# First two token tiles loaded by rows beside weight pairs on two DMA queues, and turned by TensorE, with a shorter warm-up

## Chip, cores and metric

One Trainium2 chip, one core. The metric is the device time of one execution in microseconds; lower is better. Differences of a few tenths of a per cent are the subject here, so every experiment was timed in five rounds next to the kernel before, on the same chip (except one, a single look). The groups ran on six different chips, so a comparison between groups is weaker than one within a group.

## The reference, cut to what matters

Two attention blocks read the same token matrix `x` of 2048 x 1024 (bfloat16); their outputs are mixed by a gate. Only the start matters here: the first product that the kernel forms is the value part of block B.

```python
qkv = (x @ wqkv).reshape(B, S, 3, H, Dh)...   # x: 2048 x 1024, wqkv: 1024 x 3072
q, k, v = qkv[0], qkv[1], qkv[2]              # block B's v needs x and wqkv[:, 2048:3072]
# block A: linear attention; block B: sliding, dilated window of 8; both end in @ wo
return g * a + (1 - g) * b
```

## The kernel before

Each real matmul of the opening multiplies a stationary 128 x 128 block by 512 columns (`128*128 128x512` in the profile). The kernel takes 128 tokens of `x` as the stationary block, with the features along the partitions, so it needs `x` turned: tile `xT[:, :, t*128:(t+1)*128]`. The kernel brings each of the 16 tiles by a DMA that transposes on its way. The weights of `v` come in two halves of 512 columns, and each half as four pairs of feature blocks ("weights 0-1" to "6-7", 256 KB each).

A small scheduler inside the kernel's builder orders all operations on each engine by planned costs. The scheduler's times only fix the order.

```python
WARM = 11          # matmuls on zeros, to bring TensorE's clock up

def load_x(t, prio):          # one tile of 128 tokens, transposed by the DMA
    ... e.dma_start_transpose(xT[:, :, t*128:(t+1)*128], x2[e_, r*128:(r+1)*128, :]) ...

load_x(0, 0)
load_w(0, 0, Bw, 2048, 0.1, 0, 2, "act")     # weights 0-1, ScalarE's queue
load_w(0, 0, Bw, 2048, 0.2, 2, 4, "act")
load_w(0, 0, Bw, 2048, 0.3, 4, 6)            # SyncE's queue
load_w(0, 0, Bw, 2048, 0.4, 6, 8)
for t in range(1, NT):
    load_x(t, 3 + t)
for d in range(0, 8, 2):                     # second half of the weights
    load_w(0, 1, Bw, 2560, 6.1 + 0.1 * d, d, d + 2)
# ... (cut)
for i in range(WARM):
    P.op("pe", lambda e: e.matmul(banks[7].ap(), warm[:, 0:128], warm[:, :], start=True, stop=True), 0.43, ...)
# ... (cut)
# tiles 0-3 with the first half, tiles 0-3 with the second half, tiles 4-7, ...
for t, half in [(4 * b + i, half) for b in range(NT // 4) for half in range(2) for i in range(4)]:
    step = 2 if t == 0 else 8                # tile 0 starts pair by pair
    for d in range(0, 8, step):
        o = group(bank, xs, w, [xr, ws[0].part((d, d + step), ...)], d, d + step)
    # ... eviction to SBUF and store to HBM (cut)
```

Masks for block B's window are made at the start by GpSimd and copied by VectorE; they are needed much later. The warm-up matmuls came 0.43 us apart at first, and the dense part later runs at 0.2155 us each.

Of the kernel before, what the change touches and what calls it, by code (L numbers as in the profile page):

```python
# [62 lines left out]
class Prog:  # L63
# [58 lines left out]
    def schedule(self, dma_rate=0.2e6):  # L122
        for o in self.ops:
            for d in o.deps:
                d.users.append(o)
        left = {o: len(o.deps) for o in self.ops}
        ready_at = {o: 0.0 for o in self.ops}
        free = {e: 0.0 for e in self.ENGS}
        dma_free = 0.0
        wait = {e: [] for e in self.ENGS}  # L130
        avail = {e: [] for e in self.ENGS}

        def ready(o, at):
            if o.eng == "any":

                est = []
                for e in ("act", "dve"):
                    q = sum(x[2].cost for x in avail[e] if x[0] < o.prio) + sum(x[2].cost for x in wait[e] if x[2].prio < o.prio and x[0] < at + 0.3)
                    est.append((max(free[e], at) + q + o.cost[e], e))
                o.eng = min(est)[1]  # L140
                o.fn, o.cost = o.fn[o.eng], o.cost[o.eng]
            heapq.heappush(wait[o.eng], (at, o.seq, o))

        for o in self.ops:
            if left[o] == 0:
                ready(o, 0.0)
        self.order = {e: [] for e in self.ENGS}
        mode = "m"
        done = 0
        while done < len(self.ops):  # L150
            best = None
            for e in self.ENGS:
                while wait[e] and wait[e][0][0] <= free[e]:
                    _, _, o = heapq.heappop(wait[e])
                    heapq.heappush(avail[e], (o.prio, o.seq, o))
                if avail[e]:
                    t = free[e]
                elif wait[e]:
                    t = wait[e][0][0]
                else:  # L160
                    continue
                if best is None or t < best[0]:
                    best = (t, e)
            assert best is not None, "no operation can go"
            t, e = best
            if not avail[e]:
                while wait[e] and wait[e][0][0] <= t:
                    _, _, o = heapq.heappop(wait[e])
                    heapq.heappush(avail[e], (o.prio, o.seq, o))
            _, _, o = heapq.heappop(avail[e])  # L170
            if e == "pe":

                if o.mode != mode and mode != "m":
                    near = [x for x in avail[e] if x[2].mode == mode and x[0] < o.prio + 30]
                    if near:
                        x = min(near)
                        avail[e].remove(x)
                        heapq.heapify(avail[e])
                        heapq.heappush(avail[e], (o.prio, o.seq, o))
                        o = x[2]  # L180
                if o.mode != mode:
                    t += 0.09
                mode = o.mode
            o.start = t
            o.end = t + o.cost
            free[e] = o.end
            fin = o.end
            if o.chan is not None:
                dma_free = max(dma_free, o.end) + o.lat
                fin = dma_free + o.pad  # L190
            o.pos = len(self.order[e])
            self.order[e].append(o)
            done += 1
            for u in o.users:
                lat = self.LAT[o.eng] if (u.eng != o.eng or o in u.raw) and o.chan is None else 0.0
                if u.eng == o.eng == "pe":
                    lat = 0.0
                ready_at[u] = max(ready_at[u], fin + lat)
                left[u] -= 1
                if left[u] == 0:  # L200
                    ready(u, ready_at[u])
        self.span = max(free.values())
# [914 lines left out]
def build_kernel(nc, A_x, A_wqkv, A_wo, B_x, B_wqkv, B_wo, gate_w, out):  # L1117
# [10 lines left out]
    def SB(shape, dtype, name, at=None):  # L1128
        n = SZ[dtype]
        for d in shape[1:]:  # L1130
            n *= d
        if at is None:
            at = base[0]
            base[0] += (n + 31) // 32 * 32
        uid[0] += 1
        h = nc.alloc_sbuf_tensor_at("%s_%d" % (name, uid[0]), list(shape), dtype, offset=at)
        return Tile("S", h, at, list(shape), dtype)
# [80 lines left out]
    warm = SB([128, 512], BF16, "warm", at=pk.t[2].lo)  # L1218
    gwb = SB([128, 1024], BF16, "gwb", at=pk.t[3].lo)
    xn = Ring([SB([128, 1024], BF16, "xn%d" % i, at=az.t[i].lo) for i in range(2)])  # L1220
    top_ = base[0]
    base[0] = ph
    osb = Ring([SB([128, 1024], BF16, "o%d" % i) for i in range(2)])
# [4 lines left out]

    FILL = 0.2
    PVLAG = 3  # L1230
    WARM = 11
    PASSES = 6
    mm = lambda n: max(n / 2400.0, 0.0267) + 0.0025
    act = lambda n: 0.19 + n / 1200.0
# [2 lines left out]
    def plan(seen):  # L1237
# [25 lines left out]
        def C(eng, fn, cost, writes, reads=()):  # L1263
            return P.op(eng, fn, cost, reads=reads, writes=writes, prio=-1)

        for z in vst.t:
            C("pool", lambda e, z=z: e.memset(z[:, :, 32:33], 1.0), 0.1, [z.part((0, 16), (32, 33))])
        C("pool", lambda e: e.memset(eps[:], 1e-6), 0.1, [eps.all()])
        for i, (n, offs) in enumerate(KINDS):
            for h, o in enumerate(offs):  # L1270
                m = mtmp[h]
                b0 = o + 64 * h
                C("pool", lambda e, m=m: e.memset(m[:], 1.0), 0.1, [m.all()])

                C("pool", lambda e, m=m, n=n, b0=b0: e.affine_select(out=m[:, :, 0:n], in_=m[:, :, 0:n], compare_op=ALU.is_ge, fill=0.0, base=b0,
                                                                     pattern=[[0, 2], [1, n]], channel_multiplier=-1), 0.3, [m.all()], [m.all()])
                C("pool", lambda e, m=m, n=n, b0=b0: e.affine_select(out=m[:, :, 0:n], in_=m[:, :, 0:n], compare_op=ALU.is_ge, fill=0.0, base=7 - b0,
                                                                     pattern=[[0, 2], [-1, n]], channel_multiplier=1), 0.3, [m.all()], [m.all()])
                C("dve", lambda e, m=m, n=n, h=h, i=i: e.tensor_copy(msk[i][64 * h:64 * h + 64, :, :], m[64 * h:64 * h + 64, :, 0:n]), 0.2, [msk[i].all()], [m.all()])
                P.ops[-1].prio = 1100  # L1280
        C("pool", lambda e: e.memset(zsel[:], 0.0), 0.3, [zsel.all()])

        C("dve", lambda e: e.memset(warm[:, :], 0.0), 0.15, [warm.all()])
# [22 lines left out]
        def load_x(t, prio):  # L1306
            e_, r = t // 8, t % 8
            return P.op("sp", lambda e: e.dma_start_transpose(xT[:, :, t * 128:(t + 1) * 128], x2[e_, r * 128:(r + 1) * 128, :]),  # L1308
                        1.5, writes=[xT.part((0, 8), (t * 128, (t + 1) * 128))], prio=prio, chan="x%d" % t, lat=1.3)
# [3 lines left out]
            return P.op(eng, lambda e: e.dma_start(ws[slot][:, d0:d1, half * 512:half * 512 + 512], src[:, d0:d1, c0:c0 + 512]), 0.4 + 0.2 * n,  # L1313
                        writes=[ws[slot].part((d0, d1), (half * 512, half * 512 + 512))], prio=prio, chan="w%d_%d_%d" % (slot, half, d0), lat=0.55 * n, after=after)

        load_x(0, 0)
        load_w(0, 0, Bw, 2048, 0.1, 0, 2, "act")
        load_w(0, 0, Bw, 2048, 0.2, 2, 4, "act")
        load_w(0, 0, Bw, 2048, 0.3, 4, 6)
        load_w(0, 0, Bw, 2048, 0.4, 6, 8)  # L1320
        for t in range(1, NT):
            load_x(t, 3 + t)
        for d in range(0, 8, 2):
            load_w(0, 1, Bw, 2560, 6.1 + 0.1 * d, d, d + 2)
        P.op("sp", lambda e: e.dma_start(gwb[:, :], gate_w[None, :].to_broadcast([128, D])), 0.6, writes=[gwb.all()], prio=29, chan="gw", lat=0.8)
# [46 lines left out]
        for i in range(WARM):  # L1372
            P.op("pe", lambda e: e.matmul(banks[7].ap(), warm[:, 0:128], warm[:, :], start=True, stop=True), 0.43, reads=[warm.all()], writes=[banks[7].iv], prio=-1)


        early = {(2, 0): (1, 0, Bw, 1024, 21), (4, 1): (2, 0, Bw, 0, 22), (7, 1): (1, 1, Bw, 1536, 23), (10, 1): (2, 1, Bw, 512, 24),
                 (12, 1): (3, 0, Aw, 1024, 25), (14, 1): (3, 1, Aw, 1536, 26)}
        for t, half in [(4 * b + i, half) for b in range(NT // 4) for half in range(2) for i in range(4)]:
            vt, vs = vst.next()
            xs, xr = x_tile(t)  # L1380
            bank = main.next()
            w, wr = w_half(0, half)
            step = 2 if t == 0 else 8
            for d in range(0, 8, step):
                o = group(bank, xs, w, [xr, ws[0].part((d, d + step), (half * 512, half * 512 + 512))], d, d + step)
            move(vt[:, :, 0:32], lambda bank=bank: bank.ap().rearrange("p (h d) -> p h d", d=32), 512, bank, vt.part((0, 16), (0, 32)))
            P.op("sp", lambda e, t=t, vt=vt, half=half: e.dma_start(vB_hbm[t * 128:(t + 1) * 128, half * 528:half * 528 + 528], vt[:, :, :].rearrange("p h d -> p (h d)")), 0.6, reads=[vt.all()],
                 writes=[hb(t * 128, (t + 1) * 128, half)], chan="vst%d" % vs, lat=0.5, prio=5)
            if (t, half) in early:
                load_w(*early[t, half], after=[o])  # L1390
        load_w(0, 0, Aw, 2048, 30)
        load_w(0, 1, Aw, 2560, 31)

# [424 lines left out]
```

## Time and profile before

| | before |
|---|---|
| median of the first three runs | 486.72 us (486.56 to 486.83) |
| span of the profiled run | 485.2 us |
| TensorE busy | 474.2 us |
| first real matmul | 5.54 us |
| TensorE almost without a stop from | 15.30 us |

From the page of the profile before: the span, busy time of the engines, and the shares of the chain of waits that ended last, by engine.

```profile
span 485.2 us, 10105 instructions
PE 474.2 (98%) x4339; PEld 222.8 (46%) x4403; DVE 285.2 (59%) x547; ACT 140.2 (29%) x227; POOL 5.9 (1%) x36
PE 95%; SPq 2%; issue 1%; DMA 1%; ACT 0%; DVE 0%
```

The same chain in order of time (start, duration, what). "SPq" is issuing on SyncE's queue. The chain reaches TensorE at 15.30 us and, but for short pieces, stays there; the line at 129.63 is the first score matmul, a landmark that has 568 matmuls of 512 columns ahead of it.

```profile
9.96 5.07 DMA w<-in_B_wqkv_dram
...
15.30 10.74 PE ps_all L1334 x49
...
129.63 0.53 PE ps_all L1440 x32
```

TensorE's timeline before (start, duration, engine, line, operation, operands, count; in brackets the idle time just before the group and what ended it). A group that runs on past the end of the view is cut there, as the last one here. L1373 is the warm-up, L1334 real work.

```profile
1.25 4.01 PE L1373 MATMUL ps_all<-warm 128*128 128x512 bf16 x11 [1.25 <-DVE warm L1283]
5.54 1.47 PE L1334 MATMUL ps_all<-w,xT 128*128 128x512 bf16 x6 [0.28 <-DMA xT<-in_A_x_dram]
7.25 0.60 PE L1334 MATMUL ps_all<-w,xT 128*128 128x512 bf16 x2 [0.24 <-DMA w<-in_B_wqkv_dram]
8.17 6.82 PE L1334 MATMUL ps_all<-w,xT 128*128 128x512 bf16 x30 [0.32 <-DMA xT<-in_A_x_dram]
15.30 2.97 PE L1334 MATMUL ps_all<-w,xT 128*128 128x512 bf16 x13 [0.30 <-DMA w<-in_B_wqkv_dram]
```

The first tile's transpose ends the first wait, weights end the next, and the second tile's transpose the one at 8.17. In the dense part one matmul takes about 0.2155 us, so 38 of them ahead of 15.30 us correspond to a gapless start at 15.30 - 38 x 0.2155 = 7.1 us. This "effective start" is the figure that a better opening has to lower.

SyncE's issue timeline before. A transpose holds the queue for 1.38 us and, in the group of three, for 1.6 us on average; the second half of the weights is therefore issued only from 8.31 us.

```profile
0.80 1.38 SPq L1308 DMA_TRANSPOSE xT<-in_A_x_dram  x1
2.24 1.06 SPq L1313 DMA_DIRECT2D w<-in_B_wqkv_dram  x2
3.35 4.92 SPq L1308 DMA_TRANSPOSE xT<-in_A_x_dram  x3
8.31 2.12 SPq L1313 DMA_DIRECT2D w<-in_B_wqkv_dram  x4
```

### The profile page before, as it was taken

How to read it: one execution, taken by the hardware profiler on the slowest of the kernel's cores; microseconds unless marked ns; L12 is line 12 of the kernel's file. 1: busy time of each engine (PE TensorE's matmuls, PEld its weight loads, DVE VectorE, ACT ScalarE, POOL GpSimd, SP SyncE). 2: the span in 40 equal slices, each digit the busy share in tenths (PEclk: the TensorE clock that was granted, in tenths of full speed). 3: DMA queues.
4: the chain of work that ended last, by engine and by line, in shares of the span. 5: the costliest groups of instructions: out<-in, count | busy, mean ns of one | idle time of the engine just before them, and what ended most of it. 6: DMA issues, size and time to landing. Idle time of an engine off the chain costs nothing.

```text
span 485.2 us, 10105 instructions
## 1 busy us (share of the span) xinstructions
PE 474.2 (98%) x4339; PEld 222.8 (46%) x4403; DVE 285.2 (59%) x547; ACT 140.2 (29%) x227; POOL 5.9 (1%) x36
## 2 busy tenths in 40 slices
PE   8999999999999999999999999999999999999997
PEld 3444444444444444454544554444444444444443
DVE  2121435888688888665666556496579236653434
ACT  2111121235322234334443333455532230111000
POOL 4000000000000000000000000000000000000000
PEclk9999999999999999999999999999999999999999
DMA  8999993132014459433222322820086018830212
GB/s 224 222 194 299 309 355 122 65 110 86 1 44 135 107 138 245 100 76 86 55 75 67 85 66 66 204 54 2 10 217 163 1 15 242 221 24 2 88 68 89
DMA packets 72951, 57.39 MB, mean 118 GB/s; under 512 B 37953, under 2 KB 60865, under 8 KB 72898
## 3 DMA queue, kind: packets, MB, share of 16 engines
q1 hardware_dynamic: 72210, 56.07, 44.3%
q8 instruction: 36, 0.59, 0.5%
q10 hardware_dynamic: 688, 0.59, 0.4%
q14 instruction: 17, 0.14, 0.1%
HBM read 34.49 MB, written 13.76 MB: 99 GB/s over the span
## 4 chain that ended last, share of the span: by engine, by line
PE 95%; SPq 2%; issue 1%; DMA 1%; ACT 0%; DVE 0%
PE ps_all L1334 78%; PE ps_all L1693 11%; PE ps_all L1463 2%; PE ps_all L1440 2%; SPq L1308 1%; DMA w<-in_B_wqkv_dram 1%; PE ps_all L1556 1%; SPq L1313 1%; PE ps_all L1638 0%; PE ps_all L1610 0%; ACT e L1341 0%; DVE o L1697 0%
## 5 line engine op out<-in xcount | busy, mean ns | idle before, releaser
L1334 PE MATMUL ps_all<-w,xT 128*128 128x512 bf16 x924 | 208.6, 379 | 4.5 <-issue 2.1
L1334 PE MATMUL ps_all<-xT,w 128*128 128x512 bf16 x745 | 166.3, 379 | 2.2 <-issue 1.4
L1334 PEld LDWEIGHTS ps_all<-w,xT 128*128 128x128 bf16 x960 | 91.2, 98 | 111.1 <-DMA w<-in_B_wqkv_dram 2.1
L1334 PEld LDWEIGHTS ps_all<-xT,w 128*128 128x128 bf16 x768 | 73.9, 98 | 88.7 <-issue 1.3
L1693 PE MATMUL ps_all<-w,qT 128*128 128x512 bf16 (+1 forms) x260 | 55.4, 372 | 0.2
L1693 PEld LDWEIGHTS ps_all<-w,qT 128*128 128x128 bf16 x264 | 25.9, 98 | 29.6
L1365 DVE CAST vst<-ps_all 128x512 bf16<-128x512 f32 x15 | 10.4, 694 | 43.5 <-PE ps_all L1334 43.5
L1448 ACT ACTIVATE E<-ps_all 128x1824 bf16<-128x1824 f32 (+1 forms) x18 | 30.4, 1689 | 13.4 <-PE ps_all L1440 13.4
L1345 DVE TENSOR_SCALAR e<-e 128x512 bf16<-128x512 bf16 x64 | 18.4, 290 | 26.9 <-ACT e L1343 14.0
L1697 DVE SCALAR_TENSOR_TENSOR o<-ps_all,gm,xT 128x512 bf16<-128x512 f32 (+1 forms) x25 | 18.0, 728 | 21.1 <-PE ps_all L1693 20.8
L1341 ACT ACTIVATE e<-ps_all 128x512 bf16<-128x512 f32 x32 | 19.1, 598 | 39.0 <-PE ps_all L1334 38.1
L1343 ACT ACTIVATE e<-ps_all 128x512 bf16<-128x512 f32 x32 | 19.1, 598 | 32.3 <-PE ps_all L1334 32.3
L1295 DVE TENSOR_TENSOR mx<-mx,kT 128x1024 bf16<-128x1024 bf16 x32 | 20.9, 688 | 10.9 <-ACT kT L1366 10.8
L1295 DVE TENSOR_TENSOR mx<-mx,qT 128x1024 bf16<-128x1024 bf16 x32 | 20.8, 687 | 7.9 <-ACT qT L1369 7.9
L1451 DVE TENSOR_TENSOR E<-E,msk 128x1824 bf16<-128x1824 bf16 (+1 forms) x18 | 19.9, 1104 | 7.8 <-ACT E L1448 7.4
L1366 ACT ACTIVATE vst<-ps_all 128x512 bf16<-128x512 f32 x17 | 10.2, 601 | 48.5 <-PE ps_all L1334 45.1
L1480 DVE TENSOR_TENSOR ot<-ps_all,rs 128x512 bf16<-128x512 f32 x36 | 23.3, 686 | 0.0
L1366 ACT ACTIVATE az<-ps_all 128x512 bf16<-128x512 f32 x22 | 13.2, 601 | 34.5 <-PE ps_all L1334 34.5
L1366 ACT ACTIVATE kT<-ps_all 128x512 bf16<-128x512 f32 x20 | 11.9, 597 | 37.6 <-PE ps_all L1334 37.6
L1347 DVE SCALAR_TENSOR_TENSOR pk<-ps_all,e 128x512 bf16<-128x512 f32 x32 | 22.0, 689 | 0.7
L1369 ACT ACTIVATE qT<-ps_all 128x512 bf16<-128x512 f32 x19 | 11.4, 598 | 37.4 <-PE ps_all L1334 37.3
L1369 ACT ACTIVATE xT<-ps_all,g 128x512 bf16<-128x512 f32 x10 | 6.9, 689 | 45.1 <-PE ps_all L1334 45.1
(72 smaller groups left out, 260.2 us busy)
## 6 DMA issues: line engine op xcount, KB each, us to landing
rb<-rc_hbm SPq DMA_DIRECT2D x32, 256.0 KB, 5.2
w<-in_A_wqkv_dram SPq DMA_DIRECT2D x6, 1024.0 KB, 9.0
v<-vB_hbm SPq DMA_DIRECT2D x36, 132.0 KB, 2.7
vB_hbm<-vst SPq DMA_DIRECT2D x32, 132.0 KB, 6.2
w<-in_B_wqkv_dram SPq DMA_DIRECT2D x4, 1024.0 KB, 9.5
xn<-in_A_x_dram SPq DMA_DIRECT2D x16, 256.0 KB, 2.7
out_dram<-o SPq DMA_DIRECT2D x15, 256.0 KB, 2.1
oB_hbm<-ot SPq DMA_DIRECT2D x36, 96.0 KB, 2.2
```

Of the source, the lines that this page charges most:

```text
L1295: P.op("dve", lambda e, m=m, op=op: e.tensor_tensor(m[:, 0:n], m[:, 0:n], src, op), 0.08 + n / 1920.0, reads=[m.all(), reg], writes=[m.all()],
L1334: last = e.matmul(bank.ap(), lhs(dc), rhs(dc), start=(dc == 0), stop=(dc == 7))
L1341: P.op("act", lambda e: e.activation(e_[:, :], bank.ap(), ACT.Exp), act(512), reads=[bank.iv], writes=[e_.all()])
L1343: P.op("act", lambda e: e.activation(e_[:, :], bank.ap(), ACT.Exp, accum_out=qe[:, col:col + 1]), act(512) + 0.1, reads=[bank.iv], writes= ...
L1345: P.op("dve", lambda e: e.tensor_scalar(e_[:, :], e_[:, :], 1.0, 1e-6, op0=ALU.min, op1=ALU.add), 0.25, reads=[e_.all()], writes=[e_.all()])
L1347: P.op("dve", lambda e: e.scalar_tensor_tensor(out=dst, in0=bank.ap(), scalar=0.0, in1=e_[:, :], op0=ALU.max, op1=ALU.add), dps(512), read ...
L1366: fa = lambda e: e.activation(dst, src(), ACT.Copy)
L1369: fa = lambda e: e.activation(dst, src(), ACT.Copy, scale=scale)
L1448: P.op("act", lambda e: e.activation(E[:, 0:32 * nq].rearrange("p (j q) -> p j q", j=4), ps[:, 4:8, 0:8 * nq], ACT.Exp), act(32 * nq), rea ...
L1451: P.op("dve", lambda e: e.tensor_tensor(ev(), ev(), m[:, :, :].rearrange("p r q -> p (r q)")[:, None, :].to_broadcast([128, 16, 2 * nq]), ...
L1480: P.op("dve", lambda e, r=r, bv=bv, h=h: e.tensor_tensor(o[:, 512 * h:512 * h + 512].rearrange("p (k i c) -> p k i c", k=2, c=32), bv()[:, ...
L1693: last = e.matmul(bank.ap(0, f1 - f0), qT[:, dc, t * 128:(t + 1) * 128], ws[3][:, dc, f0:f1], start=(dc == 0), stop=(dc == 7))
```

## The change

The intent is to start the real work earlier. The first two tiles are loaded plainly, by rows, and TensorE turns them itself: it multiplies each 128 x 128 block by an identity matrix, and ScalarE and VectorE copy the result from PSUM into `xT`. Row loads and weight pairs go in two queues side by side. The masks are made later, so that GpSimd can make the identity first. Because real work is expected earlier, the warm-up has six matmuls instead of eleven, and one more between the two tiles' turns. The core of the diff:

```diff
-    WARM = 11
+    WARM = 6
@@
-        load_x(0, 0)
-        load_w(0, 0, Bw, 2048, 0.1, 0, 2, "act")
-        load_w(0, 0, Bw, 2048, 0.2, 2, 4, "act")
-        load_w(0, 0, Bw, 2048, 0.3, 4, 6)
-        load_w(0, 0, Bw, 2048, 0.4, 6, 8)
-        for t in range(1, NT):
-            load_x(t, 3 + t)
+        due(load_rows(0, 0, 1024, 0, "act"), 0.45, 3.0)
+        due(load_w(0, 0, Bw, 2048, 0.1, 2, 4, "act"), 0.45, 4.6)
+        due(load_w(0, 0, Bw, 2048, 0.2, 6, 8, "act"), 0.45, 6.2)
+        due(load_w(0, 0, Bw, 2048, 0.1, 0, 2), 0.45, 3.0)
+        due(load_rows(1, 0, 1024, 0.2), 0.45, 4.6)
+        due(load_w(0, 0, Bw, 2048, 0.3, 4, 6), 0.45, 6.2)
+        for t in range(2, NT):
+            o = load_x(t, 3 + t)
+            if t < 4:
+                due(o, 1.4, 7.6 + 1.2 * (t - 2))
@@
+        for t, p in [(t, p) for t in range(2) for p in range(4)]:
+            b = banks[3 + p]
+            def turn(e, t=t, b=b, p=p):
+                for k in range(2):
+                    d = 2 * p + k
+                    last = e.matmul(b.ap(128 * k, 128 * k + 128), rows_[t][:, d * 128:(d + 1) * 128], ident[:, :], ...)
+                return last
+            o = P.op("pe", turn, 0.18, ...)
+            ... copy to xT by VectorE (p even) or ScalarE (p odd)
+            for i in range({3: 1}.get(4 * t + p, 0)):    # one more warm-up matmul
+                P.op("pe", ... warm ..., after=[o])
@@
-            step = 2 if t == 0 else 8
+            step = 2 if t == 0 or t == 1 and half == 0 else 8
@@
   (cut: the identity; the masks moved to after the 17th group; planned landing times for the scheduler)
```

`due` only tells the scheduler when a load is expected; it sets the order, not a wait.

More of the change, by code (lines that the diff above doesn't have):

```diff
@@ L188, in schedule @@
             if o.chan is not None:
-                dma_free = max(dma_free, o.end) + o.lat
-                fin = dma_free + o.pad
+                if o.lat is None:
+                    fin = max(o.end + 1.2, o.pad)
+                else:
+                    dma_free = max(dma_free, o.end) + o.lat
+                    fin = dma_free + o.pad
             o.pos = len(self.order[e])
@@ L1220, in build_kernel @@
     xn = Ring([SB([128, 1024], BF16, "xn%d" % i, at=az.t[i].lo) for i in range(2)])
+    rows_ = [SB([128, 1024], BF16, "rows%d" % i, at=az.t[2 + i].lo) for i in range(2)]
+    ident = SB([128, 128], BF16, "ident", at=er.t[0].lo)
     top_ = base[0]
@@ L1264, in C @@
             return P.op(eng, fn, cost, reads=reads, writes=writes, prio=-1)
+        C("pool", lambda e: e.memset(ident[:, :], 0.0), 0.1, [ident.all()])
+        C("pool", lambda e: e.affine_select(out=ident[:, :], in_=ident[:, :], compare_op=ALU.not_equal, fill=1.0, base=0, pattern=[[-1, 128]], channel_multiplier=1), 0.3,
+          [ident.all()], [ident.all()])
         for z in vst.t:
@@ L1268, in plan @@
         C("pool", lambda e: e.memset(eps[:], 1e-6), 0.1, [eps.all()])
-        for i, (n, offs) in enumerate(KINDS):
-            for h, o in enumerate(offs):
-                m = mtmp[h]
-                b0 = o + 64 * h
-                C("pool", lambda e, m=m: e.memset(m[:], 1.0), 0.1, [m.all()])
-                C("pool", lambda e, m=m, n=n, b0=b0: e.affine_select(out=m[:, :, 0:n], in_=m[:, :, 0:n], compare_op=ALU.is_ge, fill=0.0, base=b0,
-                                                                     pattern=[[0, 2], [1, n]], channel_multiplier=-1), 0.3, [m.all()], [m.all()])
-                C("pool", lambda e, m=m, n=n, b0=b0: e.affine_select(out=m[:, :, 0:n], in_=m[:, :, 0:n], compare_op=ALU.is_ge, fill=0.0, base=7 - b0,
-                                                                     pattern=[[0, 2], [-1, n]], channel_multiplier=1), 0.3, [m.all()], [m.all()])
-                C("dve", lambda e, m=m, n=n, h=h, i=i: e.tensor_copy(msk[i][64 * h:64 * h + 64, :, :], m[64 * h:64 * h + 64, :, 0:n]), 0.2, [msk[i].all()], [m.all()])
-                P.ops[-1].prio = 1100
         C("pool", lambda e: e.memset(zsel[:], 0.0), 0.3, [zsel.all()])
@@ L1314, in load_w, with load_rows, due @@
                         writes=[ws[slot].part((d0, d1), (half * 512, half * 512 + 512))], prio=prio, chan="w%d_%d_%d" % (slot, half, d0), lat=0.55 * n, after=after)
-        load_x(0, 0)
-        load_w(0, 0, Bw, 2048, 0.1, 0, 2, "act")
-        load_w(0, 0, Bw, 2048, 0.2, 2, 4, "act")
-        load_w(0, 0, Bw, 2048, 0.3, 4, 6)
-        load_w(0, 0, Bw, 2048, 0.4, 6, 8)
-        for t in range(1, NT):
-            load_x(t, 3 + t)
+        def load_rows(t, lo, hi, prio, eng="sp"):
+            return P.op(eng, lambda e: e.dma_start(rows_[t][:, lo:hi], x2[0, t * 128:(t + 1) * 128, lo:hi]), 0.45, writes=[rows_[t].part((lo, hi))], prio=prio, chan="xr%d_%d" % (t, lo))
+        def due(o, cost, at):
+            o.cost, o.lat, o.pad = cost, None, at
+        due(load_rows(0, 0, 1024, 0, "act"), 0.45, 3.0)
[8 more added lines that the diff above has]
+                due(o, 1.4, 7.6 + 1.2 * (t - 2))
         for d in range(0, 8, 2):
@@ L1373, in plan @@
             P.op("pe", lambda e: e.matmul(banks[7].ap(), warm[:, 0:128], warm[:, :], start=True, stop=True), 0.43, reads=[warm.all()], writes=[banks[7].iv], prio=-1)
+        for t, p in [(t, p) for t in range(2) for p in range(4)]:
[3 more added lines that the diff above has]
+                    d = 2 * p + k
+                    last = e.matmul(b.ap(128 * k, 128 * k + 128), rows_[t][:, d * 128:(d + 1) * 128], ident[:, :], start=(k == 0), stop=(k == 1), skip_group_check=True)
+                return last
+            o = P.op("pe", turn, 0.18, reads=[rows_[t].part((256 * p, 256 * p + 256)), ident.all()], writes=[b.iv], prio=-0.5 + 0.01 * p)
+            src = lambda b=b: b.ap(0, 256).rearrange("p (k s) -> p k s", k=2)
+            dst = xT[:, 2 * p:2 * p + 2, t * 128:(t + 1) * 128]
+            fn = (lambda e, dst=dst, src=src: e.activation(dst, src(), ACT.Copy)) if p % 2 else (lambda e, dst=dst, src=src: e.tensor_copy(dst, src()))
+            P.op("act" if p % 2 else "dve", fn, act(256) if p % 2 else dps(256), reads=[b.iv], writes=[xT.part((2 * p, 2 * p + 2), (t * 128, (t + 1) * 128))], prio=3 + 0.01 * p)
+            for i in range({3: 1}.get(4 * t + p, 0)):
+                P.op("pe", lambda e: e.matmul(banks[7].ap(), warm[:, 0:128], warm[:, :], start=True, stop=True), 0.43, reads=[warm.all()], writes=[banks[7].iv], prio=-0.4, after=[o])
         early = {(2, 0): (1, 0, Bw, 1024, 21), (4, 1): (2, 0, Bw, 0, 22), (7, 1): (1, 1, Bw, 1536, 23), (10, 1): (2, 1, Bw, 512, 24),
@@ L1382, in plan @@
             w, wr = w_half(0, half)
-            step = 2 if t == 0 else 8
+            step = 2 if t == 0 or t == 1 and half == 0 else 8
             for d in range(0, 8, step):
-                o = group(bank, xs, w, [xr, ws[0].part((d, d + step), (half * 512, half * 512 + 512))], d, d + step)
+                o = group(bank, xs, w, [xT.part((d, d + step), (t * 128, (t + 1) * 128)), ws[0].part((d, d + step), (half * 512, half * 512 + 512))], d, d + step)
             move(vt[:, :, 0:32], lambda bank=bank: bank.ap().rearrange("p (h d) -> p h d", d=32), 512, bank, vt.part((0, 16), (0, 32)))
@@ L1388, in plan @@
                  writes=[hb(t * 128, (t + 1) * 128, half)], chan="vst%d" % vs, lat=0.5, prio=5)
+            if (t, half) == (8, 0):
+                first = o
             if (t, half) in early:
                 load_w(*early[t, half], after=[o])
+        for i, (n, offs) in enumerate(KINDS):
+            for h, o in enumerate(offs):
+                m = mtmp[h]
+                b0 = o + 64 * h
+                P.op("pool", lambda e, m=m: e.memset(m[:], 1.0), 0.1, after=[first], writes=[m.all()])
+                P.op("pool", lambda e, m=m, n=n, b0=b0: e.affine_select(out=m[:, :, 0:n], in_=m[:, :, 0:n], compare_op=ALU.is_ge, fill=0.0, base=b0,
+                                                                     pattern=[[0, 2], [1, n]], channel_multiplier=-1), 0.3, writes=[m.all()], reads=[m.all()])
+                P.op("pool", lambda e, m=m, n=n, b0=b0: e.affine_select(out=m[:, :, 0:n], in_=m[:, :, 0:n], compare_op=ALU.is_ge, fill=0.0, base=7 - b0,
+                                                                     pattern=[[0, 2], [-1, n]], channel_multiplier=1), 0.3, writes=[m.all()], reads=[m.all()])
+                P.op("dve", lambda e, m=m, n=n, h=h, i=i: e.tensor_copy(msk[i][64 * h:64 * h + 64, :, :], m[64 * h:64 * h + 64, :, 0:n]), 0.2, writes=[msk[i].all()], reads=[m.all()])
         load_w(0, 0, Aw, 2048, 30)
```

## The prediction

> **What bounds the kernel now.** The page gives PE 474.2 of 485.2 us busy, and the chain of waits that ended last is 95% PE. In order of time, the chain's first 15.3 us are DMA issues on SP, then a weight DMA; from 15.30 us on it is PE, almost without a break. So only the opening can give time.
>
> In the PE timeline the first real matmul starts at 5.54 us, when the first DMA transpose lands. Further stops: 6.4 and 7.25 (weight pairs), 8.17 (second transpose), 14.38 and 15.02-15.30 (the second half's last pairs). 38 loads precede the last stop, so the 39th matmul starts at 15.30. At the dense rate (about 0.2155 us per 512-column matmul) this equals a gapless stream begun at 15.30 - 38 x 0.2155 = 7.1 us. I call this the effective start.
>
> Why it is late: in the SP issue timeline a transpose costs 1.25 to 2.27 us of issue and a plain load about 0.46. The second half's weights are issued only at 8.31-10.4, and the DMA rate falls under 100 GB/s around 9.6-10.8 us. Bytes start at about 2.1 us and move at 307 GB/s in 3-6 us and 258 in 6-9 us.
>
> **What the change does.** It takes two DMA transposes from the head of SP's queue and puts three plain loads on each of two queues (1.57 MB), then two transposes, then the second half's weights at about 4.9-6.9 us, 3.4 us earlier than now. [...] It adds 16 small TensorE turns (about 1 us), eight evictions of 256 columns (an estimate of 0.35-0.45 us each, from 0.60-0.69 us for 512), and moves the mask work of POOL and DVE to about 35 us, where PSUM banks give slack. PE's order after the opening is unchanged.
>
> **Cost on the path.** Estimate at 307 GB/s: the last first-half weights land at about 7.2-7.6 us, with 8 to 10 matmuls ahead of them: effective start 5.3-5.8. The third tile's transpose lands near 8.8, 16 matmuls ahead: 5.4. The second half's last pair lands at 13.3-14.5, 38 ahead: 5.1-6.3. I take 5.7, a gain of 1.4 us.
>
> Clock: six warm-up matmuls end near 3.8 us; before, the eleven changed pace from 0.43 to about 0.21 us at about 4.4. [...] Some first matmuls may now run at 0.43 us; part of that hides under DMA.
>
> **Predicted: 485.3 us, 8 in 10 between 484.4 and 486.4.** Chances: faster by over 2% 0.005, within 2% 0.99, slower by over 2% 0.005.
>
> **Right or wrong in the profile.** First real matmuls at about 5 us; first-half weights landed by 7.6; no wait for second-half weights over 0.3 us; no DMA trough near 10 us; 39th matmul at 13.5-14.2 instead of 15.30; after it, the same PE stretches shifted by a constant 1.4 us. Wrong: weight stops at 12-15 us, loads under 280 GB/s, matmuls at 0.43 us after 5 us.
>
> **What would make it wrong.** The clock stays low past 7 us (loses up to 1.5 us); two queues share so that all pairs land late together; evictions or the identity delay the turns; evictions queueing behind masks near 35 us; or bytes flow better than I think (gain over 2 us).

The sum takes 307 GB/s, the rate of the kernel before from 3 to 6 us, for both queues together (an estimate); the effective start goes from 7.1 to 5.7 us, a gain of 1.4 us, and 486.7 - 1.4 = 485.3 us.

## The result

| | before | changed |
|---|---|---|
| median, six runs each | 486.49 us | 487.73 us |
| range | 486.21 to 486.83 | 487.03 to 488.82 |
| ratio | | 1.0026, interval 1.0011 to 1.0041 |
| first real matmul (profiled run) | 5.54 us | 6.23 us |
| first score matmul | 129.63 us | 131.08 us |
| span of the profiled run | 485.2 us | 486.7 us |

A ratio is the mean time of one kernel's runs over the mean of the other's runs of the same rounds, so it is not quite the ratio of the medians. The ratios for the experiments come out when the first round, the one that was profiled, is left out of these means. The change is slower by 0.26%, inside the 2% band, and outside the predicted range.

The changed kernel's own runs already hint at something: three lie at 487.0 to 487.2 and three at 488.2 to 488.8, while before spreads over 0.6 us.

From the page of the changed kernel: span, busy time, the granted TensorE clock in 40 slices (tenths), and the chain's shares by engine.

```profile
span 486.7 us, 10207 instructions
PE 481.6 (99%) x4415; PEld 224.6 (46%) x4415; DVE 291.1 (60%) x557; ACT 137.9 (28%) x225; POOL 6.6 (1%) x38
PEclk9999999999999999999999999999999999999999
PE 98%; DMA 1%; DVE 0%; issue 0%
```

Its chain in order of time, from the first DMA to the landmark (L1387 are the turns, L1395 the extra warm-up matmul, L1339 real work, L1475 the first score matmul).

```profile
0.80 4.06 DMA rows<-in_A_x_dram
...
4.99 1.01 PE ps_all L1387 x8
6.00 0.43 PE ps_all L1395
6.43 0.85 PE ps_all L1339 x2
7.29 0.85 PE ps_all L1387 x8
8.14 122.94 PE ps_all L1339 x566
131.08 0.53 PE ps_all L1475 x32
```

The landmark came 131.08 - 129.63 = 1.45 us later than before, and the whole span is 1.5 us longer. So everything was lost in the opening, and nothing afterwards. After the first tile's rows landed at 4.9 us, the chain stays on TensorE to the landmark and beyond: TensorE is the slow part. (The chain's start of a group, 6.43 us here, counts from the end of the matmul before; the timeline, from which the table's 6.23 is taken, shows the overlapping start.) Two real matmuls took 0.85 us, twice the dense pace. The weight loads show how long that lasted (the fourth column names PE's weight loader; one load goes with each matmul, 4415 of both in the page above):

```profile
8.36 0.15 PEld L1339 LDWEIGHTS ps_all<-w,xT 128*128 128x128 bf16 x1 [0.28 <-issue]
8.79 0.15 PEld L1339 LDWEIGHTS ps_all<-w,xT 128*128 128x128 bf16 x1 [0.28 <-issue]
9.22 0.15 PEld L1339 LDWEIGHTS ps_all<-w,xT 128*128 128x128 bf16 x1 [0.28 <-issue]
9.62 0.96 PEld L1339 LDWEIGHTS ps_all<-w,xT 128*128 128x128 bf16 x5 [0.26 <-issue]
```

Loads come 0.43 us apart up to 9.62 us, then five within 0.96 us. TensorE ran at half rate until 9.6 us. Note that the clock row above shows 9 in every slice all the same: the trace's record of the clock begins only with the rise (at 9.58 us here, at 4.24 us before), and the stretch before it is drawn as full. The pace of the instructions shows the truth.

SyncE's issue timeline after. The two transposes held the queue for 5.67 us, 3.19 us of it the second one, so the second half of the weights was issued at 8.01 us.

```profile
2.30 5.67 SPq L1304 DMA_TRANSPOSE xT<-in_A_x_dram  x2
8.01 2.12 SPq L1309 DMA_DIRECT2D w<-in_B_wqkv_dram  x4
```

Landing times of the opening's loads, as issue time plus time to landing of each in the trace: rows 0 at 4.9, weights 0-1 at 5.3, weights 2-3 at 6.8, rows 1 at 6.9, weights 6-7 at 8.1 and 4-5 at 8.4 us.

Busy time and DMA rate in two stretches, first of the kernel before, then of the changed one. The columns are the stretch, its length, the busy time of PE, PEld, DVE, ACT and POOL with the instruction counts in brackets, the granted clock (drawn as full here too, see above), the DMA engines' share, and GB/s moved:

```profile
2.00:3.00 1.00, 1.00 (x4) 0.36 (x3) 0.63 (x8) 1.00 (x1) 1.00 (x6) 1.00 0.80 245
3.00:4.00 1.00, 1.00 (x4) 0.39 (x3) 0.53 (x3) 0.06 (x1) 0.79 (x5) 1.00 1.16 304
```

```profile
2.00:3.00 1.00, 1.00 (x4) 0.37 (x3) 0.63 (x8) 0.73 (x1) 0.12 (x1) 1.00 0.93 181
3.00:4.00 1.00, 0.99 (x3) 0.08 (x1) 0.06 (x1) 0.55 (x1) 0.00 (x0) 1.00 0.80 243
```

In these two microseconds the changed opening moved 0.42 MB against 0.55 MB before, although its loads were plain. One profile each: in the other two profiles of the unaltered change the first stretch reads 156 (a_again) and 119 GB/s (a_third).

**Theories.** *Clock*: six warm-up matmuls end at 4.0 us, the turns come a microsecond later, and the clock then rises late (at 9.58 us in this profile). *Arrival*: even with the clock up, the second tile's rows land together with the second load of the other queue (6.9 and 6.8 us), which is late, and hold back the real matmuls behind them. *Rivals*: the moved masks or the altered order later in the program cost the time; or loads by rows, turns and evictions are simply too dear.

### The profile page after: what moved, and what is told of

The parts are those of the page before. It is cut to its first block, busy times and chain, and to the rows that moved or that the text cites. A ratio compares the mean times of both kernels' runs of the same rounds, so it can differ in the third digit from the quotient of the medians.

```text
span 486.7 us, 10207 instructions
## 1 busy us (share of the span) xinstructions
PE 481.6 (99%) x4415; PEld 224.6 (46%) x4415; DVE 291.1 (60%) x557; ACT 137.9 (28%) x225; POOL 6.6 (1%) x38
## 4 chain that ended last, share of the span: by engine, by line
PE 98%; DMA 1%; DVE 0%; issue 0%
PE ps_all L1339 81%; PE ps_all L1728 11%; PE ps_all L1498 2%; PE ps_all L1475 2%; PE ps_all L1591 1%; DMA rows<-in_A_x_dram 1%; PE ps_all L1673 0%; PE ps_all L1387 0%; PE ps_all L1645 0%; DVE o L1732 0%; PE ps_all L1395 0%
## 5 line engine op out<-in xcount | busy, mean ns | idle before, releaser
L1339 PE MATMUL ps_all<-w,xT 128*128 128x512 bf16 x960 | 214.0, 381 | 0.0
L1339 PE MATMUL ps_all<-xT,w 128*128 128x512 bf16 x768 | 169.0, 379 | 0.0
L1339 PEld LDWEIGHTS ps_all<-w,xT 128*128 128x128 bf16 x960 | 91.9, 98 | 109.2 <-issue 1.8
L1339 PEld LDWEIGHTS ps_all<-xT,w 128*128 128x128 bf16 x768 | 73.8, 98 | 88.7 <-issue 1.3
L1371 ACT ACTIVATE vst<-ps_all 128x512 bf16<-128x512 f32 x17 | 10.2, 599 | 43.9 <-PE ps_all L1339 43.9
L1374 ACT ACTIVATE qT<-ps_all 128x512 bf16<-128x512 f32 x17 | 10.1, 597 | 40.7 <-PE ps_all L1339 40.7
L1371 ACT ACTIVATE kT<-ps_all 128x512 bf16<-128x512 f32 x16 | 9.6, 597 | 38.7 <-PE ps_all L1339 38.7
L1373 DVE TENSOR_SCALAR xT<-ps_all,g 128x512 bf16<-128x512 f32 x14 | 10.2, 748 | 17.1 <-PE ps_all L1339 17.1
```

The lines of the kernel that those rows point to most:

```text
L1339: last = e.matmul(bank.ap(), lhs(dc), rhs(dc), start=(dc == 0), stop=(dc == 7))
L1371: fa = lambda e: e.activation(dst, src(), ACT.Copy)
```

## The experiments

All were correct unless said otherwise. "Shift" below is how much later than before the first score matmul came in the profiled run (its first weight load minus 129.563 us, the same event of before; a few matmul records can be missing from a trace, the weight loads ahead of this event are complete in all). The run of before that was profiled took 486.9 us, 0.4 us above the median of its six runs, so a shift of 0 is not the usual run of before. "Clock rise" is the instant in the trace's clock record. One profile is one execution: in the third experiment nothing of the opening of TensorE or the DMAs was altered, and its shift was still +0.25 us, so smaller shifts say little.

| kernel | warm-ups | clock rise, us | shift, us | median, us (range) | before in the same rounds, us | ratio (95% interval) |
|---|---|---|---|---|---|---|
| before | 11 | 4.24 | 0 | | | |
| changed, first profile | 6 | 9.58 | +1.45 | 487.73 (487.03 to 488.82) | 486.49 | 1.0026 (1.0011 to 1.0041) |
| a_again | 6 | 4.49 | +0.09 | 488.88 (487.19 to 489.06) | 486.62 | 1.0041 (1.0027 to 1.0055) |
| a_third | 6 | 8.79 | +1.17 | 487.25 (487.00 to 488.30) | 486.96 | 1.0011 (0.9997 to 1.0025) |
| e1_warm11 | 11 | 4.32 | +0.07 | 487.20 (486.94 to 487.32) | 486.62 | 1.0009 (0.9996 to 1.0023) |
| e1_again | 11 | 4.61 | +0.28 | 487.34 (487.10 to 487.81) | 486.96 | 1.0011 (0.9997 to 1.0025) |
| e2_before_warm6 | 6 | 9.64 | +0.69 | 487.76 (487.43 to 488.31) | 486.62 | 1.0022 (1.0008 to 1.0036) |
| e3_masks_late | 11 | 4.72 | +0.25 | 486.42 (486.17 to 487.18) | 486.62 | 0.9993 (0.9979 to 1.0007) |
| e4_one_queue | 11 | 6.64 | +0.50 | 487.38 (486.99 to 488.12) | 487.05 | 1.0008 (0.9994 to 1.0021) |
| e5_rows_first | 11 | 5.61 | +0.25 | 487.60 (486.78 to 487.77) | 487.05 | 1.0007 (0.9994 to 1.0021) |
| e7_one_tile | 11 | 5.82 | +0.07 | 487.33 (486.98 to 487.45) | 487.05 | 1.0005 (0.9992 to 1.0019) |
| e6_weights_first | 11 | 4.88 | +0.56 | 488.09 (one run) | 487.05 | |
| e8_one_queue_warm6 | 6 | 6.73 | +0.18 | 487.20 (487.00 to 488.19) | 486.96 | 1.0012 (0.9999 to 1.0026) |
| e9_no_second_rows | 11 | 5.82 | +0.25 | 486.69 (486.29 to 487.31) | 486.52 | 1.0001 (0.9988 to 1.0015) |
| e10_no_rows_warm8 | 8 | 3.91 | -0.95 | 486.87 (485.99 to 487.71) | 486.44 | 1.0009 (0.9996 to 1.0023) |
| e11_warm8 | 8 | 7.00 | +0.13 | 487.18 (486.88 to 487.42) | 486.44 | 1.0012 (0.9999 to 1.0026) |
| e12_rows_first_warm8 | 8 | 4.24 | -0.39 | 486.53 (486.37 to 487.19) | 486.74 | 0.9999 (0.9986 to 1.0013) |

### The change again, unaltered (a_again, a_third)

No edit; controls within their groups.

> The changed kernel unaltered, as the control of this group. Both theories: slower than before by 0.5 to 2 us, as already seen (six runs, 487.03 to 488.82 against a median of 486.49). If the clock theory is right and the instant at which the clock rises differs from run to run, its runs spread by more than 1 us, while those of before stay within 0.7 us.

> The changed kernel unaltered, control beside the others. Clock theory: its runs fall in two groups about 1.5 us apart (near 487.2 and near 488.7), and the profile shows the slow or the fast group's clock instant (9.6 or about 4.5 us).

Measured: a_again's runs are 487.19, 487.76, 488.88, 488.90, 489.06; a_third's 487.00, 487.06, 487.25, 488.05, 488.30. The nine runs of before beside a_again spread over 0.97 us, more than the 0.7 expected, so a spread of about a microsecond alone proves little; the runs over 488 do not occur there. With the first six, eight of sixteen runs of the change are over 488.0 and seven within 487.0 to 487.3. The profiled run of a_again was one of the quick ones (487.19 us, span 485.5). TensorE's timeline of that run:

```profile
4.96 0.61 PE L1387 MATMUL ps_all<-ident,rows 128*128 128x128 bf16 x8 [0.97 <-DMA rows<-in_A_x_dram]
5.76 0.60 PE L1339 MATMUL ps_all<-w,xT 128*128 128x512 bf16 x2
6.95 0.62 PE L1387 MATMUL ps_all<-ident,rows 128*128 128x128 bf16 x8 [0.59 <-DMA rows<-in_A_x_dram]
7.40 6.85 PE L1339 MATMUL ps_all<-w,xT 128*128 128x512 bf16 x30
```

The same program, with rows landing at the same instants (4.9 and 6.9 us), now turns eight blocks in 0.61 us instead of 1.01, waits for the second tile's rows, and goes on with real matmuls from 7.40 instead of 7.93 (both by the timeline), at full rate. The three profiled runs of the unaltered change are ordered as their clock rises are: 4.49, 8.79 and 9.58 us go with spans of 485.5, 486.3 and 486.7. This is the strongest evidence for the clock, because the program is the same. It is not quite pure: a_third ran on another chip than a_again, and its two row loads landed 0.2 us later (5.1 and 7.1 us).

### Eleven warm-up matmuls in the change (e1_warm11, e1_again)

```diff
-    WARM = 6
+    WARM = 11      # planned cost scaled so that the order stays the same
```

> The changed kernel with eleven warm-up matmuls again in place of six; order of every engine otherwise the same. Clock theory (the six warm-up matmuls end at 4.0 us, before the clock has risen, and the turns and first real matmuls then run at half rate to about 9.6 us): pace changes at about 4.4 us, no matmul at 0.43 us after 5 us, and 1.2 to 1.7 us faster than the unaltered change, thus at or a little below before (0 to 0.4 us faster). Rival (the rows and weights simply land late, or the moved mask work costs, and the clock hides under that): within 0.3 us of the unaltered change, still over 0.8 us slower than before.

> The change with eleven warm-up matmuls a second time, for direct comparison with the control. Clock theory: all runs within 0.6 us of each other, near the control's fast group, 0.3 to 0.8 us slower than before. Rival (chance): two groups as in the control.

Measured: ten runs, all within 486.94 to 487.81; the group over 488 is gone. The clock theory holds in that. But the warmed change is not faster than before either: 1.0009 and 1.0011, with intervals that just include 1. The 0 to 0.4 us below before that was expected for e1_warm11 was missed, and e1_again's runs spread over 0.71 us, a little more than the expected 0.6. The chain in order of time of e1_warm11 says why. It is no longer TensorE that is slow; it waits for the second tile's rows.

```profile
1.32 5.55 DMA rows<-in_A_x_dram
...
6.92 0.62 PE ps_all L1387 x8
7.54 4.10 PE ps_all L1339 x19
```

### Six warm-up matmuls in the kernel before (e2_before_warm6)

```diff
-    WARM = 11
+    WARM = 6
```

> The kernel before with six warm-up matmuls in place of eleven, nothing else. Clock theory: first real matmuls at 5.5 us run at 0.43 us, and it is 0.3 to 1.5 us slower than before (part hides under its waits for DMA up to 8.2 us and up to 15.3 us). Rival (the warm-up count doesn't matter): within 0.2 us of before.

Measured: 1.0022, all five runs over 487.4, clock rise at 9.64 us in the profile. The weight loads of the profiled run, 0.43 us apart after the first tile had landed:

```profile
5.55 0.13 PEld L1334 LDWEIGHTS ps_all<-w,xT 128*128 128x128 bf16 x2 [2.46 <-DMA xT<-in_A_x_dram]
...
9.37 0.15 PEld L1334 LDWEIGHTS ps_all<-w,xT 128*128 128x128 bf16 x1 [0.28 <-issue]
```

So the shorter warm-up alone costs the kernel before 1.1 us by the medians, without rows, turns or a second queue. It is the one part of the change whose harm shows by itself.

### Only the masks moved (e3_masks_late)

The mask loop of the kernel before was moved to where the change has it; nothing else.

> The kernel before with only the mask work of POOL and DVE moved to after the seventeenth group, as the change has it. Both of my theories: within 0.2 us of before. A rival in which the moved masks delay evictions and so TensorE: over 0.3 us slower, with a TensorE wait near 35 to 45 us.

Measured: 0.9993, no difference. The rival of the masks falls.

### One queue in place of two (e4_one_queue)

```diff
-        due(load_rows(0, 0, 1024, 0, "act"), 0.45, 3.0)
-        due(load_w(0, 0, Bw, 2048, 0.1, 2, 4, "act"), 0.45, 4.6)
-        due(load_w(0, 0, Bw, 2048, 0.2, 6, 8, "act"), 0.45, 6.2)
-        ... three loads on SP
+        # all six on "sp": rows 0, weights 0-1, rows 1, weights 2-3, 4-5, 6-7
```

with eleven warm-up matmuls and planned landing times to match.

> The change with eleven warm-up matmuls and its six opening loads on SP's queue alone, in the order rows 0, weights 0-1, rows 1, weights 2-3, 4-5, 6-7. Sharing theory (two queues side by side split one bandwidth, so the second tile's rows land together with the weights of the other queue, at 6.9 us): rows 0 land at 3.5 to 4.2 us, rows 1 at 5.2 to 5.9, the last weights at 7.8 to 8.3, and TensorE is dense from about 6.2 us; 0.4 to 1.0 us faster than the change with eleven warm-up matmuls on two queues (e1), that is 486.0 to 486.8 and 0 to 0.6 us below before. Rival (row loads are slow by themselves, whatever the queue): rows 1 land after 6.5 us and the time is within 0.2 us of e1.

Measured: the landings were as the sharing theory has them: rows 0 at 3.9, rows 1 at 5.8, the last weights at 8.0 us (8.2 on two queues, in e1). So two queues side by side do make the second tile's rows land a microsecond later than one queue does. The time was not 0.4 to 1.0 us better, though: that expectation was missed. The clock rose at 6.64 us in the profiled run, the eleven warm-up matmuls ran at half rate to 5.9 us, and rows that had lain ready since 3.9 us waited behind them. The warm-up itself had become the wait. One run of the five was over 488 (488.12); it was not profiled.

### Both row loads first (e5_rows_first)

```diff
+        # "act": rows 0, weights 0-1, 4-5;  "sp": rows 1, weights 2-3, 6-7
```

> As e1, two queues, but the two row loads first, one at the head of each queue, then weights 0-1 and 2-3, then 4-5 and 6-7. Sharing theory: both row loads land at about 4.9 us, two weight pairs at 6.8, the last two at 8.2; TensorE dense from 6.8 us; 0.2 to 0.6 us faster than e1. Rival (row loads are slow by themselves): both row loads land after 5.5 us, the weights after 7.2, time within 0.2 us of e1 or slower.

Measured: 1.0007, not faster than e1; missed. Rows landed at 5.0 and 5.2 us, as the sharing theory says within 0.3 us, and the first two weight pairs at 6.1 and 6.6, earlier than expected. Again the clock rose late (5.61 us) and the warm-up ran to 5.8 us.

### Only the first tile by rows (e7_one_tile)

```diff
-        for t in range(2, NT):
+        for t in range(1, NT):       # the second tile comes by DMA transpose again
```

> As e1, but only the first tile by rows; the second comes by DMA transpose again. Half of the turns and evictions. Arrival theory: the second tile's transpose lands at 8.0 to 8.6 us with eight matmuls ahead of it, so TensorE is dense from there with an effective start 0.3 to 0.7 us earlier than e1; 0.2 to 0.7 us faster than e1. Rival (the turns and evictions cost nothing and arrival order does not matter): within 0.2 us of e1.

Measured: 1.0005, a shift of +0.07; missed. The weight loads of the profiled run:

```profile
8.28 5.84 PEld L1338 LDWEIGHTS ps_all<-w,xT 128*128 128x128 bf16 x28 [0.21 <-DMA xT<-in_A_x_dram]
14.45 0.11 PEld L1338 LDWEIGHTS ps_all<-w,xT 128*128 128x128 bf16 x2 [0.34 <-DMA w<-in_B_wqkv_dram]
15.13 0.76 PEld L1338 LDWEIGHTS ps_all<-w,xT 128*128 128x128 bf16 x5 [0.56 <-DMA w<-in_B_wqkv_dram]
```

The second tile's transpose landed at 8.2 us as expected, with eight matmuls ahead of it. But three transposes again kept the second half of the weights from being issued before 8.50 us, and the waits near 15 us of the kernel before came back.

### Weights first on both queues (e6_weights_first)

```diff
+        # "act": weights 0-1, rows 0, weights 4-5;  "sp": weights 2-3, rows 1, weights 6-7
```

> One look, for the slow start of the DMA traffic. As e1, two queues, but each begins with a weight pair and the rows come second. In the traces of the change the two queues together move about 160 GB/s from 2.0 to 3.25 us[...]. If two plain loads at once are slow to start whatever they read: about 160 GB/s again in that stretch, weights landing at 4.7 to 5.3 us. If it is the row loads that are slow: over 280 GB/s, both weight pairs landing by 4.2 us. The total time is not the question (matmuls of the second tile wait behind the last weights here).

Measured, one look: 234 GB/s from 2 to 3 us and 344 from 3 to 4 us; the first weights landed at 4.5 and 4.8 us. That lies between the two expectations in the first microsecond and clearly above the change in the second (243). From 2.00 to 3.25 us, the stretch that the expectation names, e6 moved 253 GB/s and the kernel before 253 as well. In e5, where both queues begin with rows, the two stretches of one microsecond moved 195 and 207 GB/s; on one queue that begins with rows, the first of them moved 226 (e4) and 244 (e8). So, by single profiles, the slow start goes with row loads that run beside another queue rather than with two queues as such, or with rows as such. What in them is slow was not found; this is left open.

### One queue and six warm-up matmuls (e8_one_queue_warm6)

e4 with `WARM = 6`, so that nothing stands before the turns when the rows land at 3.9 us.

> One queue as in e4, but six warm-up matmuls again, so that the turns of the first tile do not stand behind warm-up work: in e4 the clock rose only at 6.6 us, the eleven warm-up matmuls ran at half rate to 5.9 us, and rows that had landed at 3.9 us waited two microseconds for them. Here the rows land at 3.9, TensorE is busy almost without a gap from 1.25 us, so the clock rises by 6.7 us at the latest. Theory (the clock's instant and the late second tile together ate the gain): first turns at 3.9 to 4.1 us, effective start 0.5 to 1.0 us earlier than before, 0.4 to 1.0 us faster than before. Rival (the opening is bound by the bytes of the second half of the weights anyhow, or the clock rises at 9.6 us again): within 0.4 us of before, or slower.

Measured: 1.0012, not faster; missed. The turns did start at 3.88 us. But the clock rose at 6.73 us, TensorE worked at half rate until then, and weights 2-3 landed at 7.4 us, 5.2 us after their issue (in e4 they landed at 6.5). When they came, only two real matmuls were done. One run was again over 488 (488.19). Why the same load took nearly a microsecond longer than in e4 was not settled; transposes of the third and fourth tile were moving at the same time.

### The wait for the second tile's rows taken away (e9_no_second_rows, e10_no_rows_warm8, with its control e11_warm8)

These two kernels give a wrong result on purpose. The order on every engine is that of e1.

```diff
-        due(load_rows(1, 0, 1024, 0.2), 0.45, 4.6)
+        due(load_rows(1, 0, 16, 0.2), 0.45, 4.6)        # 16 columns of 1024
-   last = e.matmul(..., rows_[t][:, d * 128:(d + 1) * 128], ident[:, :], ...)
+   last = e.matmul(..., rows_[0][:, d * 128:(d + 1) * 128], ident[:, :], ...)
```

e9 has eleven warm-up matmuls, e10 eight. e11 is the correct change with eight.

> Wrong result on purpose. The change with eleven warm-up matmuls (e1), every engine in the same order, but the second tile's load brings 16 of its 1024 columns only, and its turns read the first tile's rows. That takes away the wait for the second tile's rows (6.9 us in e1, the last wait before TensorE is dense) and 0.26 MB. Arrival theory: the next waits are the weights, landing at 6.0 to 6.5 and 7.2 to 7.8 us; with the clock up by 5 us the effective start is 0.5 to 1.0 us earlier than in e1, and the time 0.4 to 1.0 us below e1's, about 486.3, 0 to 0.5 below before. If the clock rises only near 6.6 us in the profiled run, half of that. Rival (something else than these rows, such as the turns and evictions, sets the start): effective start within 0.2 us of e1's.

> Wrong result on purpose. As e9 (no wait for the second tile's rows), with eight warm-up matmuls, which end by 4.7 us even at half rate, as the first tile's rows land; in e9's profiled run the clock rose at 5.8 us, so eleven ran to 5.9 us and hid what the missing rows give. Arrival theory: first turns at about 4.6 to 4.8 us; with the clock up by 5 us the effective start is 0.5 to 1.0 us earlier than in e1 (e1: 6.73 counted at the weight loads), with the clock up near 6 us 0.2 to 0.6 earlier; the time 0.3 to 0.8 us below e11. Rival: effective start and time as in e11, within 0.2 us.

> The change, correct, with eight warm-up matmuls instead of six or eleven. Clock theory: activity reaches from 1.25 to 4.7 us and goes on with the turns at 4.9, so the clock rises by 6.7 us at the latest in every run and never near 9 us; no run of the slow group (over 488), median 486.8 to 487.3, dense from about 7.4 us because the second tile's rows land at 6.9. So not faster than before by 0.3 us or more. Rival (only the count of eleven, four microseconds of it, is enough): two groups as in the control, up to 488.9.

Measured: e9's median was 486.69 and its ratio 1.0001, but its profiled run had a late clock (5.82 us) and showed no earlier start: on its own this was inconclusive. In e10's profiled run the clock rose at 3.91 us. Its chain in order of time:

```profile
0.80 3.75 DMA rows<-in_A_x_dram
...
4.68 0.61 PE ps_all L1387 x8
...
6.53 5.61 PE ps_all L1339 x26
```

TensorE is dense from 6.53 us instead of 7.54 in e1, the first score matmul comes 0.95 us earlier than in before, and the span is 484.3 us with a time of 485.99, the lowest. So with the clock up in time, the arrival of the second tile's rows, with the 0.26 MB that they add, was what held the opening; the turns and evictions, all still there, were not. Two limits: the 16 columns that remain landed at 5.74 instead of 6.87 us, so the wait was brought forward rather than abolished, and the other five loads of the opening came 0.2 to 1.2 us earlier too, so the wait and the bytes are not separated. The ratios do not show it: e10's five runs spread over 1.7 us and its ratio is 1.0009 beside e11's 1.0012, where 0.3 to 0.8 us had been expected. These ratios leave out the profiled run, e10's quickest; with it the medians are 0.31 us apart. The timings settle nothing here. I put the spread down to the clock's instant, but only one of the five runs was profiled, so that is an inference.

e11's five runs lie within 486.88 to 487.42 and none is over 488, although the clock rose only at 7.00 us in its profiled run, later than the 6.7 that the expectations of e8 and e11 gave as the latest (an estimate; with eleven warm-up matmuls the latest rise had been e4's 6.64; e8 itself had 6.73). With activity from 1.25 us nearly without a gap, a late clock costs little there: the second tile's rows landed at 6.6 us, TensorE at half rate was ready for most of their turns at about 7.0, and real matmuls went on at 7.44, against 7.38 in e1.

### Rows first, both tiles turned, eight warm-ups (e12_rows_first_warm8)

```diff
+    WARM = 8
+        # "act": rows 0, weights 2-3, 6-7;  "sp": rows 1, weights 0-1, 4-5
```

> A correct version that follows from e5, e10 and e11: eight warm-up matmuls, both row loads at the heads of the two queues, then weights 0-1 (SP) and 2-3 (ACT), then 4-5 and 6-7, both tiles turned before the first real matmul. Arrival theory: rows land at 5.0 to 5.3 us, two weight pairs at 6.1 to 6.6, TensorE dense from 6.2 to 6.6 us, effective start 0.3 to 0.6 us earlier than in e1 and 0.2 to 0.5 us faster than before (486.0 to 486.3 beside 486.5), no run over 488. Rival (the bytes of the opening cannot be put in an order that beats before): effective start 6.6 to 7.0 at the weight loads as in e5, time 0.2 to 0.8 us slower than before.

Measured: correct, no run over 488, dense from 6.65 us by the chain, shift -0.39 us: the opening is better than before, by what was expected. The time is not: 0.9999, no difference. In the profiled run (one of its two slower ones, 487.19) the gain was given back late. Its chain near the end:

```profile
415.42 7.27 DMA out_dram<-o
...
422.78 0.76 DVE o L1732
...
423.59 20.89 PE ps_all L1339 x96
```

An output buffer came free late, VectorE's eviction waited for it, and TensorE for VectorE. By the weight loads, e12, 0.39 us ahead of before at the landmark and still 0.30 at 397 us, is 0.14 us behind after this point. This is one profile; whether the quicker runs (486.37 to 486.53) miss that stall is not known. No version beats the kernel before beyond noise.

## Why the prediction was wrong, point by point

- **"So only the opening can give time": right.** From the first score matmul to the end, before took 355.61 us and the change 355.65 us in the profiles. The loss sits in the first 16 us.
- **"Effective start 5.3-5.8 ... I take 5.7": this is the step that failed, by a wrong count of the matmuls ahead of the last wait.** I assumed "8 to 10 matmuls ahead" of the last first-half weights. The second tile's turns stand after two real matmuls in TensorE's list, and they wait for rows that land at 6.9 us. So only two real matmuls were ahead of the wait that counted. From e1's chain: the turns after that wait end at 7.54 us, and 7.54 - 2 x 0.2155 = 7.1 us, the effective start of the kernel before. With the clock up, the warmed change (e1, a_again) started where before does: shifts of +0.07 and +0.09, an effective start of about 7.2 us. e10, nearly without those rows, gained 1.0 us over e1 in its profile: most of the missing 1.4. The 39th matmul, predicted at 13.5 to 14.2 us, thus came at about 15.4 in the warmed change and 16.7 in the first profile (estimates: 15.30 plus the shift).
- **"The last first-half weights land at about 7.2-7.6": wrong.** They landed at 8.1 and 8.4. I used 307 GB/s from the first byte; the traces show 181 and 243 in the first two microseconds. My own warning, "loads slower than 280 GB/s", was met. I also treated the loads as if they came one after another. Two queues side by side finish their second loads together (6.8 and 6.9), which is late for the one that is needed first; on one queue the rows landed at 5.8 us (e4). The prediction's own list of risks has this, "two queues share so that all pairs land late together"; the sum left it out. The one rate that the sum takes for both queues agrees with the runs in this, that the last first-half weights landed at 8.2 us on two queues (e1) and at 8.0 on one (e4); what it leaves out is the order of arrival.
- **The clock: mechanism named, size far too small.** I wrote that some matmuls may run at half rate and that "part of that hides under DMA", and gave the clock up to 1.5 us only as a risk. In half of sixteen runs the change was 1 to 2 us slower than its quick group, and the profiled runs tie that to a rise at 8.8 to 9.6 us. With the first matmul at 1.25 us, the rise came at 4.24 to 6.64 us with eleven warm-up matmuls and at 3.91, 4.24 and 7.00 us with eight; in the four profiles with six and then a gap of 0.97 to 1.56 us it came at 4.49, 8.79, 9.58 and 9.64 us, and with six and no such gap (e8) at 6.73 us. The term was there, but at zero in the sum; it should have been about 0.7 us on average, an estimate from half the runs times the 1.4 us that separate the first profile and a_again.
- **"Second half's weights at about 4.9-6.9 us": wrong, and harmless.** They were issued from 8.01 us, because one transpose held the queue for 3.19 us, while other loads were under way; the quickest one in the same kernel held it for 1.23 us. They were still not waited for, as the prediction said, since the start was late. The trough of the DMA rate that the prediction puts at about 9.6 to 10.8 us in the kernel before is shorter in the trace, some 9.6 to 10.2 us (63 GB/s, and 295 from 10.2 to 10.8 us); the changed kernel has none there (250 GB/s from 9 to 10 us), as predicted.
- **Turns about 1 us, evictions 0.35 to 0.45 us: right.** Both were estimates. Measured: an eviction took 0.43 us on VectorE and 0.38 on ScalarE; 16 turns took 1.7 us at half rate and about 0.9 at full rate.
- **Masks near 35 us harmless: right.** e3 shows no cost (ratio 0.9993), and from 30 to 40 us TensorE was busy for 9.95 us in the kernel before and for 10.00 us in the changed one.

What stays open: why row loads beside another queue start slowly; and the 0.4 to 0.6 us by which the medians of the warmed change still lie over before, while its opening in the profiles is only 0.07 to 0.28 us later. The intervals include zero, and part may be the yardstick: the profiled run of before was itself 0.4 us slower than its median.

## What to carry to other kernels

In this kernel TensorE started dense work when the load that was waited for last had landed (in e1 the second tile's rows at 6.9 us, dense from 7.54 us; in e10, with that load cut short, dense from 6.53 us), and what counted was how much work stood ahead of that wait in its list (two matmuls, where 8 to 10 had been counted). So write down the landing time of each load and the instructions ahead of it, not the sum of the bytes. When a change cuts warm-up work because "real work comes sooner", check in the trace that TensorE stays busy from the first warm-up matmul until the real work. Here a gap of 0.97 to 1.56 us after six warm-up matmuls went with a clock rise at 8.79 to 9.64 us in three profiles of four (4.49 us in the fourth), while the latest rise without such a gap was at 7.00 us (e11); half of the changed kernel's sixteen runs were over 488 us. Look at every run's time, not at a median: two groups a microsecond apart pointed here to a state that one profile shows only by luck.
